# First MLP of an attention and two-MLP kernel: results leave and return by ScalarE's DMA queue, work between products becomes chains

## The chip, the cores and the metric

The kernel runs on one core of a Trainium2 chip. The metric is the device time of one execution in microseconds (us), the median of several runs. TensorE (PE in the profile) multiplies matrices and accumulates in PSUM banks; VectorE (DVE) and ScalarE (ACT) do element-wise passes; SyncE (SP) issues DMAs. Each engine works through its own queue of instructions in order, and an engine whose next instruction waits holds everything behind it.

## The reference

```python
attn = phi(q) @ (phi(k).T @ v) / den        # linear attention, 4 x 8 heads, 576 tokens
x = attn as 2304 x 512
h = x @ w_in;  g = np.maximum(0.01 * h, h);  x = g @ w_out          # first MLP, 512 -> 2048 -> 512
h = x @ w_in2; g = h * np.tanh(softplus(h)); out = g @ w_out2       # second MLP, same sizes
```

Weights come as 64-bit floats and the result is to have 32-bit accuracy.

## The kernel before

**Products.** A product of 32-bit floats is made of three matmuls of high and low halves (`three`, L96 to L99: high with high, high with low, low with high). The halves come from a ScalarE copy (`high`, the L201 and L93 passes) and a VectorE subtraction (`low`, L205 and L94). Weights are first converted from 64-bit floats: a load into a `stage` place (L124, two places, 512 KB each, by SP), a clamp and a shift on VectorE (L135, L137), a scale on ScalarE (L141), two joining passes on VectorE (L146 into a scratch tile `e`, L150 into `c`). There are two `c` places. A converted block is used at once or stored to DRAM (`scr`, L159, SP) and fetched later (`fc`, L164, SP).

**First MLP, in-stage.** Blocks f = 0 to 7 of w_in and two halves of the tokens make 16 items. An item is seven products of six 128x512 matmuls each in the manner of Strassen (`cycle`, L860); per f there is also a product for the 256 left-over tokens (`c_item`, 24 matmuls of 256 columns). Between products stand small passes on which the next product waits: copies of banks by ScalarE (`seed_y` L657, `keep_p7` L660) and sums of banks by VectorE (L704, L709). A finished result goes through `leaky` (L694): a ScalarE pass into one of six 256 KB places (`g`), then a DMA to DRAM (L698, `gd<-g`, SP). There are 72 results.

**First MLP, out-stage.** Five blocks of tokens (512, 512, 256, 512 and 512 columns) in 16, 16, 8, 16 and 16 steps. A step (`emit_y`, L922) is 12 matmuls of 512 columns (24 of 256 in the short block) on one result, which comes back by a DMA (`load_g`, L913, `raw<-gd`, SP) and is cut into `gh` (ScalarE) and `gl` (VectorE) by `split_g`, two steps ahead. The loads stand four steps ahead, in the last block two steps ahead. In the last block each step also fetches and splits a w_out block of the second MLP (`swap`, L1126), and the second MLP's first products begin.

**What sets the order.** Weight work for later stands in one list of pieces (`piece`, L608; `conv_pieces`, L800; `w_pieces`, L790). After some products `work` (L618) takes pieces from the head of the list while tokens last: four calls in a `cycle`, one in an out-stage step, each call worth 1.75 to 2.4 us of VectorE work. `need` (L622) takes pieces until the one that a product wants is out. All DMAs of these stages stand in SP's queue, in program order.

Of the kernel before, what the change touches and what calls it, by code (L numbers as in the profile page):

```python
# [23 lines left out]
def attention_two_mlps_kernel(  # L24
# [39 lines left out]
    NC = B * LEFT  # L64

# [41 lines left out]
    class Loads:  # L107


        def __init__(self, units):  # L110
            self.units, self.at, self.stage = units, 0, {}

        def load(self, ahead=1):
            while self.at < len(self.units) and len(self.stage) <= ahead:
# [10 lines left out]
                self.stage[which, m, x] = stg  # L125

    def conversion(u, then):
# [64 lines left out]
    def w_sums(f):  # L192
        c0, c1 = kept[0, 2 * f, 0], kept[0, 2 * f + 1, 0]
        l0, r0, l1, r1 = c0[:, 0:E], c0[:, E:], c1[:, 0:E], c1[:, E:]
        for o, x, op, y in ((r1, l1, ALU.add, r1), (l1, l0, ALU.subtract, l1),
                            (l0, r1, ALU.subtract, l0), (r0, r0, ALU.subtract, l0)):
            nc.vector.tensor_tensor(out=o, in0=x, in1=y, op=op)
# [42 lines left out]
    with tc.manual_schedule():  # L240
# [253 lines left out]
        def attention(n):  # L494
# [48 lines left out]
            if n == PAIRS - 1:  # L543
# [9 lines left out]
        l1_order = {}  # L553
        for f in range(3, NF):
            part = -(-len(others) // (NF - f))
            l1_order[f] = others[:part] + [(0, 2 * f, 0), (0, 2 * f + 1, 0)]
            others = others[part:]
        l2_order = out1[DIRECT + STORED:] + [(1, m, 0) for m in range(M)] + out2[AHEAD:]
        loads = Loads([u for u, _ in att_units.values()] + [u for x in l1_order.values() for u in x] + l2_order)
        conv = {n: conversion(u, then(u)) for n, (u, then) in att_units.items()}  # L560
# [45 lines left out]
        gd, ready, bg, tokens, rate, free = {}, {}, [], [0.0], [1.9], set()  # L606

        def piece(cost, f, mark=None, gate=None):  # L608
            bg.append((cost, f, gate))
            if mark is not None:  # L610
                ready[mark] = f

        def next_piece():
            cost, f, gate = bg.pop(0)
            assert gate is None or gate in free
            f()
            return cost
# [70 lines left out]
        turn = [0]  # L688

        def staged():  # L690
            turn[0] += 1
            return work6(("ta", "gh", "gl")[turn[0] % 3], "g", F32)

        def leaky(key, h):  # L694
            g = staged()
            nc.scalar.activation(out=g, in_=h, func=AF.Prelu, alpha=0.01)
            gd[key] = dr.tile([P, MAIN], F32, name="gd%d_%d" % key)
            nc.sync.dma_start(out=gd[key], in_=g)  # L698

        def tail5(n):  # L700
# [4 lines left out]
            leaky((2 * x["f"] + 1, 2 * x["sb"] + 1), c)  # L705
# [52 lines left out]
        def high_piece(part):  # L758
            piece(0.0, lambda: high(part()))

        def low_piece(cost, part, mark):
            piece(cost, lambda: low(part()), mark)

        c_part = lambda: cw + [XC]
        x1 = lambda o: (lambda: x_part(1, o))
        high_piece(c_part)
        low_piece(1.22, c_part, ("x", "c", 0))
        high_piece(x1(B11))
        piece(0.69, lambda: nc.vector.tensor_tensor(out=XC[:, 0:2], in0=XC[:, 2:4], in1=XC[:, 0:2], op=ALU.subtract))
        high_piece(d_part)  # L770
        low_piece(1.22, x1(B11), ("x", 1, B11))
        low_piece(0.69, d_part, ("x", "c", 1))
        high_piece(x1(B22))
        piece(1.22, lambda: x_sum(1, T1))
        piece(1.22, lambda: x_sum(1, T3))
        high_piece(x1(T3))
        low_piece(1.22, x1(B22), ("x", 1, B22))
        piece(1.22, lambda: x_sum(1, T2))
        high_piece(x1(T2))
        low_piece(1.22, x1(T3), ("x", 1, T3))  # L780
# [416 lines left out]
```

## Time and profile before

| | us |
|---|---|
| median of three runs (1031.61 to 1036.34) | 1032.63 |
| profiled execution, its own time | 1036.78 |
| its span | 1034.9 |
| TensorE busy | 972.4 |
| VectorE busy | 727.4 |
| ScalarE busy | 528.4 |

The stages in the profiled execution: attention to 176.6 us, the in-stage of the first MLP to 395.4, its five out blocks to 446.7, 493.6, 518.0, 565.0 and about 645, then the second MLP to the end. A busy TensorE is not one at its peak: the granted clock has two levels, and a stretch after idle time can stand at the lower one.

### The profile page before, as it was taken

To read this page: it belongs to the slowest core of one execution; us is meant where nothing else is said; L and a number is where in the kernel's file an instruction comes from. 1 tells how busy PE (TensorE), PEld (TensorE's weight loads), DVE (VectorE), ACT (ScalarE), POOL (GpSimd) and SP (SyncE) were. 2 spreads that over 40 slices of the span, in tenths; PEclk is the share of its full clock that TensorE was granted. 3 is DMA by queue.
4 is the path that set the end of the run, shared out by engine and by line. 5 is a ranking of instruction groups with operands and counts; after the bars stand their busy time and mean duration, and the time that the engine had idled before them with its cause. 6 is when DMAs were issued, how large, how long until landed. Compare 5 with 4: busy or idle time off the path is not lost.

```text
span 1034.9 us, 16987 instructions
## 1 busy us (share of the span) xinstructions
PE 972.4 (94%) x6645; PEld 810.9 (78%) x6645; DVE 727.4 (70%) x1282; ACT 528.4 (51%) x898; POOL 68.7 (7%) x36
## 2 busy tenths in 40 slices
PE   8999999978968898999999879999999999999998
PEld 7889998766757786767977547888888988888886
DVE  7888995757665313777876224987886888868975
ACT  6888896644444333444443223645544555445543
POOL 4444431000000000000000000000000000000000
PEclk9999999999989899999999889999999999999999
DMA  7534411237765325656577222000100100000001
GB/s 196 142 86 119 128 46 43 83 132 223 233 194 181 136 112 176 213 181 202 194 259 229 96 91 79 11 1 1 41 1 1 41 1 21 1 1 35 7 0 41
DMA packets 84367, 102.88 MB, mean 99 GB/s; under 512 B 28992, under 2 KB 53952, under 8 KB 84288
## 3 DMA queue, kind: packets, MB, share of 16 engines
q1 hardware_dynamic: 83552, 101.41, 30.8%
q8 instruction: 52, 0.85, 0.4%
q10 hardware_dynamic: 736, 0.39, 0.1%
q14 instruction: 27, 0.22, 0.1%
HBM read 72.42 MB, written 29.36 MB: 98 GB/s over the span
## 4 chain that ended last, share of the span: by engine, by line
PE 58%; DVE 11%; DMA 9%; ACT 5%; issue 4%; SPq 1%; ACTq 0%; DVEq 0%
PE b L97 10%; PE b L98 9%; PE b L99 9%; PE a L97 9%; PE a L98 9%; PE a L99 9%; DMA scr<-c 4%; DMA raw<-gd 4%; DVE e L146 2%; DVE c L150 2%; DVE gl L94 2%; ACT gh L93 2%; DVE c L135 1%; PE outs L432 1%; PE kvp L409 1%
## 5 line engine op out<-in xcount | busy, mean ns | idle before, releaser
L98 PE MATMUL a<-win,wi 128*128 128x512 f32 (+1 forms) x320 | 117.7, 368 | 0.0
L99 PE MATMUL a<-win,wi 128*128 128x512 f32 (+1 forms) x320 | 117.7, 368 | 0.0
L97 PE MATMUL a<-win,wi 128*128 128x512 f32 (+1 forms) x320 | 117.7, 368 | 0.0
L99 PE MATMUL b<-wo,gl 128*128 128x512 f32 x288 | 112.2, 390 | 0.4 <-DVE gl L1044 0.4
L97 PE MATMUL b<-wo,gh 128*128 128x512 f32 x288 | 112.2, 389 | 0.0
L98 PE MATMUL b<-wo,gh 128*128 128x512 f32 x288 | 112.2, 389 | 0.0
L94 DVE TENSOR_TENSOR gl<-raw,gh 128x512 fp32r<-128x512 f32 x72 | 49.6, 689 | 83.3 <-ACT gh L93 83.2
L97 PE MATMUL b<-gh,wo 128*128 128x512 f32 (+1 forms) x192 | 72.7, 379 | 16.7 <-ACT gh L93 16.3
L141 ACT ACTIVATE c<-c 128x512 f32<-128x512 f32 x64 | 40.5, 633 | 90.9 <-DVE c L135 89.4
L1026 ACT ACTIVATE gh<-u 128x512 fp32r<-128x512 f32 x72 | 45.5, 633 | 69.8 <-PE b L98 63.0
L93 ACT ACTIVATE gh<-raw 128x512 fp32r<-128x512 f32 x72 | 44.8, 623 | 70.2 <-DMA raw<-gd 57.1
L98 PE MATMUL b<-gl,wo 128*128 128x512 f32 (+1 forms) x192 | 73.7, 384 | 4.0 <-DVE gl L94 3.7
L392 POOL PARTITION_ALL_REDUCE qm<-qd x32 | 68.5, 2189 | 90.8 <-ACT qd L387 77.2
L99 PE MATMUL b<-gh,wo 128*128 128x512 f32 (+1 forms) x192 | 71.1, 370 | 0.1
L1053 ACT ACTIVATE r<-e,two 128x512 f32<-128x512 f32 x72 | 51.7, 718 | 37.0 <-DVE e L1038 37.0
L97 PEld LDWEIGHTS a<-win,wi 128*128 128x128 f32 x320 | 60.3, 188 | 10.3
L98 PEld LDWEIGHTS a<-win,wi 128*128 128x128 f32 x320 | 60.3, 188 | 10.3
L99 PEld LDWEIGHTS a<-win,wi 128*128 128x128 f32 x320 | 60.3, 188 | 10.1
L1022 ACT ACTIVATE e<-a 128x512 f32<-128x512 f32 x72 | 43.0, 597 | 47.1 <-PE a L99 26.3
L99 PEld LDWEIGHTS b<-wo,gl 128*128 128x128 f32 x288 | 54.1, 188 | 12.5 <-DVE gl L1044 1.2
L97 PEld LDWEIGHTS b<-wo,gh 128*128 128x128 f32 x288 | 54.1, 188 | 11.0
L98 PEld LDWEIGHTS b<-wo,gh 128*128 128x128 f32 x288 | 54.1, 188 | 10.9
(223 smaller groups left out, 2364.1 us busy)
## 6 DMA issues: line engine op xcount, KB each, us to landing
gd<-g SPq DMA_DIRECT2D x72, 256.0 KB, 2.0
raw<-gd SPq DMA_DIRECT2D x72, 256.0 KB, 4.0
stage<-in_moe_w_in_dram SPq DMA_DIRECT2D x32, 512.0 KB, 3.9
stage<-in_moe_w_out_dram SPq DMA_DIRECT2D x32, 512.0 KB, 4.1
scr<-c SPq DMA_DIRECT2D x22, 256.0 KB, 4.3
fc<-scr SPq DMA_DIRECT2D x19, 256.0 KB, 2.7
qn<-in_q_dram SPq DMA_DIRECT2D x16, 256.0 KB, 3.9
vmain<-in_v_dram SPq DMA_DIRECT2D x32, 128.0 KB, 3.0
```

Source lines behind the costliest of these rows:

```text
L93: nc.scalar.activation(out=hi, in_=src, func=AF.Copy)
L94: nc.vector.tensor_tensor(out=lo, in0=src, in1=hi.bitcast(F32), op=ALU.subtract)
L97: nc.tensor.matmul(out=o, lhsT=wh_, rhs=xh, start=start, stop=False, **kw)
L98: nc.tensor.matmul(out=o, lhsT=wh_, rhs=xl, start=False, stop=False, **kw)
L99: nc.tensor.matmul(out=o, lhsT=wl_, rhs=xh, start=False, stop=stop, **kw)
L141: nc.scalar.activation(out=box["c"], in_=box["c"], func=AF.Copy, scale=2.0 ** -112)
L146: nc.vector.scalar_tensor_tensor(out=e, in0=stg[:, :, 1], scalar=-(1 << 31), in1=stg[:, :, 0], op0=ALU.bitwise_and, op1=ALU.bitwise_or)
L150: nc.vector.scalar_tensor_tensor(out=c.bitcast(I32), in0=c.bitcast(I32), scalar=3, in1=e, op0=ALU.logical_shift_left, op1=ALU.bitwise_or)
L392: nc.gpsimd.partition_all_reduce(qm, qd, P, bass_isa.ReduceOp.absmax)
L1022: nc.scalar.activation(out=e0, in_=h0, func=AF.Exp)
L1026: nc.scalar.activation(out=hi2, in_=u2, func=AF.Copy)
L1053: nc.scalar.activation(out=r0, in_=e0, func=AF.Ln, bias=two)
```

## The change

- `leaky` no longer issues its DMA; the DMA is put aside (`sent`) and issued on ScalarE's queue at the next call of `work`, one product later. `load_g` issues on ScalarE's queue too, six steps ahead instead of four (the first six loads come before the last item of the in-stage); in the last block two at a time every second step, the last six into `stage` places.
- `work` is called once per product (seven times per item, twice per out-stage step). The list of pieces becomes a queue of chains; each call lets every open chain (at most four) do one stage at most, and tokens are worth 1.3 us per call, 1.0 in the out-stage.
- `c` has three places. A clamp is placed at the earliest three calls after the load of its block was issued (`landed`). The scratch tile `e` is gone: L146's result is written into the `stage` place, which is given back after L150 instead of after L146.
- 31 conversions stand in the in-stage instead of 24: for each f three blocks go to the store beside the two of w_in. The last two of the seven conversions in the attention stage now store w_out blocks; they kept w_in blocks. Blocks of w_out that the first MLP needs are fetched from the store, four of them before the handover between the stages. Two calls of `drain` empty the queue: at the handover, and one step before the last block.
- Up to three pairs `gh`, `gl` are made ahead instead of two. `swap` keeps three fetches in flight instead of two.

```diff
+    CS, LAND = 3, 3
...
-            c = box["c"] = gp.tile([P, DM], F32, tag="c", name="c")
+            c = box["c"] = gp.tile([P, DM], F32, tag="c", name="c", bufs=CS)
...
             stg, c = box["s"], box["c"]
-            e = gp.tile([P, DM], I32, tag="w1", name="e", bufs=1)
-            nc.vector.scalar_tensor_tensor(out=e, in0=stg[:, :, 1], scalar=-(1 << 31), in1=stg[:, :, 0],
+            e = stg[:, :, 0]
+            nc.vector.scalar_tensor_tensor(out=e, in0=stg[:, :, 1], scalar=-(1 << 31), in1=e,
                                            op0=ALU.bitwise_and, op1=ALU.bitwise_or)
+            nc.vector.scalar_tensor_tensor(out=c.bitcast(I32), in0=c.bitcast(I32), scalar=3, in1=e,
+                                           op0=ALU.logical_shift_left, op1=ALU.bitwise_or)
             del loads.stage[u]
             loads.load()
-            nc.vector.scalar_tensor_tensor(out=c.bitcast(I32), in0=c.bitcast(I32), scalar=3, in1=e,
-                                           op0=ALU.logical_shift_left, op1=ALU.bitwise_or)
             then(c)
...
-    def fetch(u, tag="c"):
-        c = gp.tile([P, DM], F32, tag=tag, name="f" + tag, **({"bufs": 1} if tag == "w1" else {}))
+    def fetch(u):
+        c = gp.tile([P, DM], F32, tag="c", name="f", bufs=CS)
         nc.sync.dma_start(out=c, in_=scr[u])
         return c
...
-        DIRECT, STORED, AHEAD = 3, 5, 6
-        att_units = {1: ((0, 0, 0), keep), 2: ((0, 1, 0), keep), 5: ((0, 0, 1), store), 7: ((0, 2, 0), keep),
-                     8: ((0, 3, 0), keep), 15: ((0, 4, 0), keep), 16: ((0, 5, 0), keep)}
-        out1, out2 = [(0, m, 1) for m in range(1, M)], [(1, m, 1) for m in range(M)]
-        others = out1[:DIRECT + STORED] + out2[:AHEAD]
...
+        ATT = {1: ((0, 0, 0), keep), 2: ((0, 1, 0), keep), 5: ((0, 0, 1), store), 7: ((0, 2, 0), keep),
+               8: ((0, 3, 0), keep), 15: ((0, 1, 1), store), 16: ((0, 2, 1), store)}
+        HERE, EARLY, EACH = 4, 1, 3
+        out1, out2 = [(0, m, 1) for m in range(M)], [(1, m, 1) for m in range(M)]
+        spare = out1[3:] + out2
...
+        for f in range(2, NF + 1):
+            part = EARLY if f == 2 else EACH
+            pair = [(0, 2 * f + i, 0) for i in range(2) if f < NF]
+            l1_order += pair + spare[:part] if f == 2 else spare[:part] + pair
+            spare = spare[part:]
+        l2_order = [(1, m, 0) for m in range(M)] + spare
...
-        gd, ready, bg, tokens, rate, free = {}, {}, [], [0.0], [1.9], set()
...
-        def work(share=1.0):
-            tokens[0] = min(tokens[0] + share * rate[0], 2.0 * rate[0])
-            while bg and tokens[0] > 0 and (bg[0][2] is None or bg[0][2] in free):
-                tokens[0] -= next_piece()
+        gd, free, undone, pos, tokens, rate = {}, set(), set(), [0], [0.0], [1.3]
+        queue, active, sent = [], [], []
+        loads.pos = pos
...
+            def step(self, force):
+                x = self.stages[0]
+                if pos[0] < self.at + x.after and not force:
+                    return
+                if (x.gate is not None and x.gate not in free) or (x.ok is not None and not x.ok(force)):
+                    return
+                if x.cost > 0 and tokens[0] <= 0 and not force:
+                    return
+                self.at = pos[0]
+                tokens[0] -= x.cost
+                self.stages.pop(0)
+                x.f()
+                undone.discard(x.mark)
...
+        def work(force=False):
+            pos[0] += 1
+            while sent:
+                sent.pop(0)()
+            tokens[0] = min(tokens[0], 0.0) + rate[0]
+            for x in list(active):
+                x.step(force)
+            active[:] = [x for x in active if x.stages]
+            while queue and len(active) < 4 and not any(x.open() for x in active) and (force or queue[0].begin <= pos[0]):
+                x, n = queue[0], len(queue[0].stages)
+                x.at = -9
+                x.step(force)
+                if len(x.stages) == n:
+                    return
+                queue.pop(0)
+                if x.stages:
+                    active.append(x)
...
-            f = ready.pop(mark, None)
-            while f is not None and any(f is x for _, x, _ in bg):
-                next_piece()
+            while mark in undone:
+                work(True)
...
+        def drain():
+            while queue or active:
+                work(True)
...
+        turn, stage_tags = [0], [("ta", "gh", "gl")]
         def staged():
             turn[0] += 1
-            return work6(("ta", "gh", "gl")[turn[0] % 3], "g", F32)
-        def leaky(key, h):
-            g = staged()
+            return work6(stage_tags[0][turn[0] % len(stage_tags[0])], "g", F32)
+        def leaky(key, h, g=None):
+            g = staged() if g is None else g
             nc.scalar.activation(out=g, in_=h, func=AF.Prelu, alpha=0.01)
             gd[key] = dr.tile([P, MAIN], F32, name="gd%d_%d" % key)
-            nc.sync.dma_start(out=gd[key], in_=g)
+            sent.append(lambda: nc.scalar.dma_start(out=gd[key], in_=g))
...
-        def conv_pieces(u, then):
-            c, s, j = conversion(u, then)
-            piece(0.85, lambda: (c(), s()))
-            piece(1.38, j)
...
+        def room(force=False):
+            return len(held) < CS or held[-CS][0]
...
+        def landed(u):
+            def ok(force):
+                loads.load()
+                return room() and u in loads.stage and (force or pos[0] >= loads.when[u] + LAND)
+            return ok
...
+        def to_store(u):
+            box, st_ = conv_stages(u)
+            j = st_[2]
+            f = j.f
+            j.f = drop(box, lambda: (f(), store(u)(box["out"])))
+            chain(*st_)
...
+        def from_store(u, begin=0):
+            box = {}
+            def get():
+                box["h"] = hold()
+                box["out"] = fetch(u)
+            h, l = into_home(u, box)
+            h.after = LAND
+            chain(Stage(0.0, get, ok=room, last=True), h, l, begin=begin)
...
-            t = rawt[s] = place("a%d" % (s % RAW), F32, MAIN, name="raw") if s < LAST else work6("ta", "raw")
-            nc.sync.dma_start(out=t, in_=gd[steps[s][2]])
+            if s < LAST + 10:
+                t = place("a%d" % (s % RAW), F32, MAIN, name="raw")
+            else:
+                if (s - LAST) % 2 == 0:
+                    raw2[0] = gp.tile([P, 2, MAIN], F32, tag="stage", name="raw2")
+                t = raw2[0][:, s % 2]
+            rawt[s] = t
+            nc.scalar.dma_start(out=t, in_=gd[steps[s][2]])
...
+        def g_tag(s):
+            return s % 3 == 2 and s < NS - 6
...
-            hi, lo = work6("gh", "gh"), work6("gl", "gl")
+            hi, lo = ((work6("ta", "gh", F32R), work6("ta", "gl", F32R)) if g_tag(s) else (work6("gh", "gh"), work6("gl", "gl")))
...
+        def splits(s):
+            while s + 3 >= len(gs) < NS:
+                x = len(gs)
+                before = [y for y in gs if g_tag(y) == g_tag(x)][-1 if g_tag(x) else -2:]
+                if len(before) == (1 if g_tag(x) else 2) and before[0] > s:
+                    return
+                gs.append(x)
+                split_g(x)
...
+                if n == len(it) - 1:
+                    for s in range(6):
+                        load_g(s)
...
-        while bg:
-            next_piece()
-        for s in range(4):
-            load_g(s)
+        drain()
+        for u in out1[HERE:]:
+            from_store(u)
...
+        rate[0] = 1.0
...
             h, l = home[1, m, 1] = home_of((1, m, 1))
             split(h, l, box2.pop(m))
-            x = m + 2 if m + 2 <= M - 3 else m + 1
-            if M - 3 != m + 1 and x < M:
-                box2[x] = fetch(out2[x], "c" if x < M - 3 else "w1")
+            if m + CS < M:
+                box2[m + CS] = fetch(out2[m + CS])
...
         def l2_step(s):
-            emit_y(s)
-            if s < LAST - 4:
-                load_g(s + 4)
-            elif s >= LAST - 2:
-                load_g(s + 2)
-            split_g(s + 2)
+            emit_y(s, 0, 1)
             work()
+            emit_y(s, 2, 3)
+            splits(s)
+            if s < LAST + 4:
+                load_g(s + 6)
+            elif (s - LAST) % 2 == 0:
+                load_g(s + 6)
+                load_g(s + 7)
+            work()
+            if s >= LAST:
+                swap(s - LAST)
         for s in range(NS):
-            if s == LAST - 2:
-                while bg:
-                    next_piece()
+            if s == LAST - 1:
+                drain()
```

SP's queue in the second half of the in-stage; `stage` is a load of a 64-bit block, `scr` a store of a converted one, `gd` a result. Before:

```order
L698 DMA gd_3_3570<-g 128x512
L164 DMA fc<-scr_0_1_1314 128x512
L124 DMA stage<-in_moe_w_out_dram 128x1024
L698 DMA gd_2_3605<-g 128x512
L124 DMA stage<-in_moe_w_in_dram 128x4x256 x2
L698 DMA gd_3_3654<-g 128x512
```

After:

```order
L161 DMA scr_6_1_3703<-c 128x512
L125 DMA stage<-in_moe_w_out_dram 128x1024 x3
L161 DMA scr_7_1_3833<-c 128x512
L125 DMA stage<-in_moe_w_in_dram 128x4x256
L161 DMA scr_8_1_3886<-c 128x512
```

The results are gone from SP's queue; loads and stores of weights alone are left.

VectorE's queue near the end of the in-stage: 14 conversion passes stand in a row ahead of a sum of banks (`g<-b,z`, `b<-b,z`) on which TensorE waits; `z` is the copy that `keep_p7` makes, `x_...` a low half of a weight. Before, the end of that row:

```order
L146 SCALAR_TENSOR_TENSOR e<-stage 128x512
L150 SCALAR_TENSOR_TENSOR c<-c,e 128x512
L135 TENSOR_SCALAR c<-stage 128x512
L137 TENSOR_SCALAR stage<-stage 128x512
L704 TENSOR_TENSOR g<-b,z_74 128x512
L709 TENSOR_TENSOR b<-b,z_75 128x512
```

After, at the same sums:

```order
L747 TENSOR_TENSOR g<-b,z_74 128x512
L207 TENSOR_TENSOR x_0_4184<-c,x_0_4184 128x512
L137 TENSOR_SCALAR c<-stage 128x512
L139 TENSOR_SCALAR stage<-stage 128x512
L752 TENSOR_TENSOR b<-b,z_75 128x512
L207 TENSOR_TENSOR x_1_4198<-c,x_1_4198 128x256
L199 TENSOR_TENSOR c<-c 128x256 x4
L148 SCALAR_TENSOR_TENSOR stage<-stage 128x512
L150 SCALAR_TENSOR_TENSOR c<-c,stage 128x512
```

The conversions are cut up between the sums.

The last out block: SP's queue before, where each return of a result (`raw<-gd`) stands behind a fetch:

```order
L164 DMA fc<-scr_6_1_6119 128x512
L913 DMA raw<-gd_3_4145 128x512
L164 DMA fc<-scr_7_1_6166 128x512
L913 DMA raw<-gd_3_4408 128x512
L164 DMA fc<-scr_8_1_6195 128x512
```

and ScalarE's queue after:

```order
L1017 DMA raw_6578<-gd_3_4606 128x512
L1017 DMA raw_6578<-gd_3_4567 128x512
L94 ACTIVATE wo<-f 128x512
L94 ACTIVATE gh<-raw 128x512
```

The returns stand in pairs on ScalarE; SP's queue keeps the fetches alone.

## Rows read from the trace of the kernel before

**Rows 1.** Stretches by stage: start:end length, busy us (instructions) of PE, PEld, DVE, ACT, POOL; clock.
```profile
176.60:395.40 218.80, 189.70 (x856) 155.90 (x852) 114.38 (x197) 95.76 (x166) 0.00 (x0) 0.92 0.49 163
395.40:446.70 51.30, 46.80 (x193) 35.45 (x194) 33.90 (x60) 21.10 (x37) 0.00 (x0) 1.00 0.54 180
446.70:493.60 46.90, 45.60 (x194) 35.32 (x192) 37.21 (x66) 21.66 (x37) 0.00 (x0) 1.00 0.59 192
493.60:518.00 24.40, 23.61 (x193) 23.12 (x192) 20.63 (x38) 11.78 (x21) 0.00 (x0) 1.00 0.61 201
518.00:565.00 47.00, 45.93 (x194) 35.48 (x193) 33.21 (x62) 17.20 (x31) 0.00 (x0) 1.00 0.78 253
565.00:644.90 79.90, 65.58 (x230) 47.39 (x230) 26.79 (x44) 23.12 (x42) 0.00 (x0) 0.89 0.28 92
645.00:1000.00 355.00, 354.65 (x1655) 297.15 (x1654) 290.38 (x490) 181.61 (x291) 0.00 (x0) 1.00 0.04 12
```

**Rows 2.** TensorE's waits in the in-stage: us in total, times, longest.
```profile
PE b L97 <- ACT b L657: 14.8, 5, 5.4
PE b L97 <- DVE g L704: 9.9, 4, 4.8
PE a L97 <- DVE g L704: 2.3, 1, 2.3
```

**Rows 3.** TensorE's waits in the first four out blocks (395.4 to 565).
```profile
PE b L97 <- ACT gh L93: 4.3, 3, 2.3
```

**Rows 4.** TensorE's waits in the last out block (565 to 644.9).
```profile
PE b L97 <- ACT gh L93: 12.0, 10, 1.8
```

**Rows 5.** Timeline: start, length; first matmuls of two stretches twelve matmuls apart.
```profile
219.85 0.39 PE L97 MATMUL a<-v,a 128*128 128x512 f32 x1
...
222.57 0.39 PE L97 MATMUL b<-s,x 128*128 128x512 f32 x1
```

**Rows 6.** Ten microseconds after a stall, columns as in rows 1.
```profile
230.00:240.00 10.00, 9.74 (x32) 7.29 (x32) 8.55 (x16) 5.55 (x11) 0.00 (x0) 0.72 0.66 200
```

**Rows 7.** Timeline of one stall in the in-stage; in brackets idle before and its releaser.
```profile
257.01 0.43 DVE L135 TENSOR_SCALAR c<-stage 128x512 f32<-128x512 f32 x1 [1.81 <-DMA scr<-c]
...
257.47 0.63 ACT L141 ACTIVATE c<-c 128x512 f32<-128x512 f32 x1 [3.46 <-DVE c L135]
...
259.62 0.79 PE L97 MATMUL b<-v,x 128*128 128x512 f32 x1 [3.69 <-ACT b L657]
```

**Rows 8.** VectorE's waits in the in-stage.
```profile
DVE c L135 <- DMA scr<-c: 16.5, 10, 2.3
```

**Rows 9.** Waits of SP's queue, 185 to 640.
```profile
SPq L698 <- ACT g L696: 125.7, 59, 5.8
SPq L164 <- DVE wo L94: 50.2, 11, 5.4
```

**Rows 10.** Timeline of one step of the last block.
```profile
587.33 0.32 SPq L164 DMA_DIRECT2D fc<-scr  x1
587.70 0.42 SPq L913 DMA_DIRECT2D raw<-gd  x1
590.75 0.63 ACT L93 ACTIVATE gh<-raw 128x512 fp32r<-128x512 f32 x1 [3.73 <-DMA raw<-gd]
```

**Rows 11.** DMA issues from 190 to 345: count, KB each, median us to landing.
```profile
stage<-in_moe_w_out_dram SPq DMA_DIRECT2D x14, 512.0 KB, 4.3
```

**Rows 12.** DMA issues on ScalarE's queue at the program's start.
```profile
0.75 0.39 ACTq L276 DMA_DIRECT2D kn<-in_k_dram  x1
...
3.24 1.38 ACTq L289 DMA_DIRECT2D ql<-in_q_dram  x2
```

**Rows 13.** Groups of VectorE's instructions in the in-stage: busy us, mean ns.
```profile
L146 DVE SCALAR_TENSOR_TENSOR e<-stage 128x512 int32<-128x512 int32 x24 | 16.6, 692 | 0.7
...
L135 DVE TENSOR_SCALAR c<-stage 128x512 f32<-128x512 f32 x24 | 10.2, 423 | 16.5 <-DMA scr<-c 16.5
```

**Rows 14.** Groups of ScalarE's instructions in the in-stage.
```profile
L696 ACT ACTIVATE g<-b 128x512 f32<-128x512 f32 x31 | 18.4, 595 | 19.4 <-PE b L99 17.4 <-ACT g L696 1.5 <-ACT x L201 0.2
```

More of the change, by code (lines that the diff above doesn't have):

```diff
@@ new lines, in attention_two_mlps_kernel, with __init__, open @@
+        class Chain:
+            def __init__(self, stages, begin=0):
+                self.stages, self.begin, self.at = list(stages), begin, pos[0]
+                undone.update(x.mark for x in stages if x.mark is not None)
+            def step(self, force):
[11 more added lines that the diff above has]
+                undone.discard(x.mark)
+            def open(self):
+                return any(not x.last for x in self.stages)
@@ L800, in conv_pieces, with row, f @@
-        def conv_pieces(u, then):
-            c, s, j = conversion(u, then)
-            piece(0.85, lambda: (c(), s()))
-            piece(1.38, j)
+        def row(cost, *todo, mark=None):
+            def f():
+                for t in todo:
+                    t()
+            return Stage(cost, f, mark)
+        hi_ = lambda part: (lambda: high(part()))
+        lo_ = lambda part: (lambda: low(part()))
+        sum_ = lambda o: (lambda: x_sum(1, o))
+        d_sub = lambda: nc.vector.tensor_tensor(out=XC[:, 0:2], in0=XC[:, 2:4], in1=XC[:, 0:2], op=ALU.subtract)
@@ new lines, in attention_two_mlps_kernel, with hold, conv_stages, c_ @@
+        held = []
+        def room(force=False):
+            return len(held) < CS or held[-CS][0]
+        def hold():
+            held.append([False])
+            return held[-1]
+        def landed(u):
[3 more added lines that the diff above has]
+            return ok
+        def conv_stages(u, last=True):
+            box = {}
+            c, s, j = conversion(u, lambda x: box.update(out=x))
+            def c_():
+                box["h"] = hold()
+                c()
+            return box, [Stage(0.85, c_, ok=landed(u), last=last), Stage(0.0, s), Stage(1.38, j)]
@@ new lines, in drop, with g, w_chain, got @@
+        def drop(box, f=None):
+            def g():
+                if f is not None:
+                    f()
+                box["h"][0] = True
+            return g
+        def w_chain(f, begin):
+            b0, (c0, s0, j0) = conv_stages((0, 2 * f, 0))
+            b1, (c1, s1, j1) = conv_stages((0, 2 * f + 1, 0), last=False)
+            sums = [lambda: w_sums(f, slice(0, 2)), lambda: w_sums(f, slice(2, 4))]
+            p = lambda i: (lambda: w_part(f, i))
+            def got():
+                kept[0, 2 * f, 0], kept[0, 2 * f + 1, 0] = b0["out"], b1["out"]
+            def both(*fs):
+                def g():
+                    for x in fs:
+                        x()
+                return g
+            c1.after = 1
+            chain(c0, Stage(0.85, both(s0.f, c1.f), ok=c1.ok, last=False), Stage(1.38, both(j0.f, s1.f)), Stage(1.38, both(j1.f, got)),
+                  Stage(0.0, hi_(p(0)), gate=(f - 2, 0)),
+                  Stage(0.69, both(lo_(p(0)), hi_(p(1))), ("w", f, 0), gate=(f - 2, 1)),
+                  Stage(1.27, both(lo_(p(1)), sums[0]), ("w", f, 1)),
+                  Stage(0.84, both(sums[1], hi_(p(2))), gate=(f - 2, 2)),
+                  Stage(0.69, both(drop(b1, lo_(p(2))), hi_(p(3))), ("w", f, 2), gate=(f - 2, 3)),
+                  Stage(0.69, drop(b0, lo_(p(3))), ("w", f, 3)), begin=begin)
@@ L842, in out_w @@
             return home[u]
-        w_pieces(2)
-        from_store((0, 0, 1))()
-        for f in range(3, NF):
-            for u in l1_order[f]:
-                if u[2] == 0:
-                    conv_pieces(u, keep(u))
-                elif u in out1[:DIRECT]:
-                    direct(u)
-                else:
-                    conv_pieces(u, store(u))
-            w_pieces(f)
+        begin = {2: 13, 3: 28}
+        begin.update((f, 22 + 16 * (f - 3)) for f in range(4, NF))
+        todo = list(l1_order)
+        while todo:
+            u = todo.pop(0)
+            if u[2] == 0:
+                todo.pop(0)
+                w_chain(u[1] // 2, begin[u[1] // 2])
+            else:
+                to_store(u)
+        for m in range(HERE):
+            from_store(out1[m])
         def used(n, *parts):
@@ L882, in cycle @@
             head2(n)
+            work()
             tail3(n - 1)
@@ L933, in emit_y @@
                           start=(m == 0), stop=(m == M - 1))
+            if KD - 1 not in ds:
+                return
+            del gt[s]
             if ms[-1] == M - 1:
```

164 lines of the change are left out of this document (59 added, 105 removed).

## The prediction

> **What bounds the kernel now.** I read the stretches by stage first: each row gives a stage's length beside its TensorE busy time and clock [rows 1]. From 645 to 1000 us TensorE is busy for 354.65 of 355.00 us at full clock; the change leaves that stage alone, so it keeps its time. The first MLP, 176.6 to about 645, is another matter: in-stage and last block have both idle time and a clock under 1. I price each stage by what its matmuls need back to back. Twelve matmuls of 512 columns, one step, take 222.57 - 219.85 = 2.72 us, 0.2267 each [rows 5]. For 256 columns I take the short block's busy time, 23.61 / 193 = 0.122 [rows 1].
>
> - In-stage: by the code 108 products of 6 matmuls and 8 of 24 narrow ones: 648 x 0.2267 + 192 x 0.122 = 170.3, with 1.5 us set aside for its 16 other matmuls 171.8, against 218.80. Excess 47.0.
> - First four out blocks: 3 x 192 x 0.2267 + 192 x 0.122 = 154.0 against 51.30 + 46.90 + 24.40 + 47.00 = 169.6. Excess 15.6.
> - Last block: 230 x 0.2267 = 52.1 against 79.90. Excess 27.8.
>
> Together 90.4 us, all that better order can win. Which waits make it up? In the in-stage TensorE waits 14.8 us for the ScalarE copy that seeds a bank and 9.9 + 2.3 for the VectorE sum [rows 2]; in the last block 12.0 for `gh` [rows 4]; in the four blocks between 4.3 for it [rows 3]. Idle time alone is less than the excess: the in-stage's idle is 218.80 - 189.70 = 29.1. The other 18 are the clock: in the ten microseconds from 230 us TensorE was busy for 9.74, yet 32 matmuls ran instead of 10 / 0.2267 = 44, at a granted 0.72, a mix of the levels 2.4 and 1.2 GHz [rows 6]. So a stall is paid more than once here, and its removal returns more than its idle time.
>
> One stall shows the mechanism [rows 7]. VectorE's clamp waits 1.81 us for a store to read its `c` place; ScalarE's scale waits 3.46 us for that clamp; the seed copy stands behind the scale in ScalarE's queue, and TensorE waits 3.69 us for it. The store was itself late in SP's queue, whose results wait 125.7 us in all for their ScalarE pass [rows 9]. VectorE waited for such stores ten times, 16.5 us [rows 8]. In the last block the same happens on SP alone: the fetch waits for a VectorE pass over its place (50.2 us over 11 fetches), the result's return stands behind the fetch, is issued at 587.70, and its `gh` begins at 590.75, after 3.73 us of idle [rows 9, 10].
>
> **The change part by part.**
>
> *Results' DMAs to ScalarE.* 72 out and 72 back leave SP. A DMA issue on ScalarE took 0.39 us for one and 1.38 for two [rows 12]; so 0.39 to 0.69. Per f (14 products and one narrow item, 14 x 1.36 + 24 x 0.122 = 22.0 us of TensorE) ScalarE does some 22 passes (9 results, 4 copies, 5 scales, 4 halves) at about 0.6 [rows 14] = 13.2, and 9 issues add 3.5 to 6.2: 16.7 to 19.4 of 22.0. It fits, and since the issue is put off by one product, the pass it reads is long done: price nothing, with 2.6 us per f as cover. What is queued behind such an issue is the next seed copy, so 0.69 us of its slack goes. In the out-stage a step has 0.6 for `gh`, up to 1.2 for weights and 0.69 for the load, 2.5 of 2.72, and `gh` is made two steps ahead.
>
> *Chains, one stage per product.* This removes the cause of [rows 7] and of the waits for the sum: of 14 conversion passes in a row, about 14 / 2 x (0.423 + 0.692) = 7.8 us [rows 13] ahead of a sum, at most a few stay between two sums. VectorE's load per f is now five conversions of 2 x 0.423 + 2 x 0.692 = 2.23, so 11.1; lows 3 x 0.69 + 0.42 = 2.5; four sums of weights 1.7; four sums of banks 2.8: 18.1 of 22.0 us. Half widths are priced as the clamp's 0.423, an estimate.
>
> *The added wait.* A clamp now follows its load by three calls, some 4.1 us of TensorE work (3 x 1.36), while a load took 4.3 to land as a median [rows 11]. Queued behind a clamp that waits are the sums on VectorE, and the scale and then the seed copy on ScalarE. Price from both sides: nothing (the load lands in time), or 2 us, the worst wait of a clamp before, near the 2.3 of [rows 8]. I take 0.2 us per conversion, since the distance misses the median by that. 18.1 + 1 = 19.1 of 22.0 still fits, but not evenly, since some products carry two conversion passes and a sum; I leave 10 of the 47.0 us: about 1.2 us for each of six f, and 3 for the beginning, where the halves of the other tokens are made.
>
> *Three `c` places, `e` in place.* A `c` place comes back one conversion later, so the 16.5 us of [rows 8] go. The `stage` place comes back 0.69 us later, one L150 [rows 13]; that is in the 0.2 us above.
>
> *Handover.* `drain` puts a fetch and its split on ScalarE in a row ahead of the last item's passes, without lead. A fetch is like the return in [rows 10]: 590.75 - 587.70 = 3.05, and 0.63 for the split. I add 4 us.
>
> *Out blocks.* 33 conversions become 26, and two calls of 1.0 per step bound VectorE to about 2 us of weights and 0.69 for `gl` per 2.72 us. That is nearly full; the lead of two to three steps hides single lumps. I leave 2 us in the first block and 3 in the other three, 5 of 15.6.
>
> *Last block.* The return no longer stands behind the fetch, and is issued six steps ahead; nothing of the loop of [rows 10] is left. VectorE has 0.69 for `gl`, 0.69 for a fetched half and a few splits: half of a step. I leave 2 of 27.8 us.
>
> A rule speaks against half of this. The last block is where only the queue changes, and there the DMA share is 0.28 [rows 1], so what was short was a turn in SP's queue, not the engines that move data. The Trainium skill (DMA: Bandwidth & Descriptors, "Issuing engines are not separate DMA queues") says that transfers started by several engines run on the same 16 DMA engines, and that starting them on more engines saves only the time of the issue. By that the last block would keep its excess; the 50.2 us in [rows 9] are a wait at the issue, before any transfer, which that rule doesn't count.
>
> Sum: 10 + 4 + 5 + 2 = 21 of 90.4 stay, 69.4 go. 1036.78 - 69.4 = 967.4 for a profiled execution; that of before lay 4.15 above the median of its runs, so **963**.
>
> **The rivals.**
>
> *A, VectorE becomes the bound.* Each of the 31 conversions of the in-stage waits the full 2 us for its load. Then VectorE has 18.1 + 10 = 28.1 per f against 22.0, six f lose 37 instead of 10, and the out blocks 8 instead of 5 (loads 3 calls ahead there too). Excess 37 + 4 + 8 + 2 = 51, saved 39.4: 993. For it: the distance is under the median landing time, and two `stage` places allow no earlier load. Against it: SP's queue is rid of the results, and landing is counted from issue with DMA shares of 0.49 to 0.78, part of which are lumps that even spacing takes away. Range 976 to 1000.
>
> *B, the queue is worth nothing.* The returns land no earlier, since the transfers are what is late: 26 of the last block's excess stay, the rest goes as forecast. 10 + 4 + 5 + 26 = 45, saved 45.4: 987. That is the rule above; against it speak the share of 0.28 and the 3.05 us that one return took once it was issued.
>
> *C, slower: ScalarE pays the issues.* If an issue holds ScalarE until its transfer has been taken over, at x us each, an f costs 13.2 + 9x against 22.0 and a step 1.5 + x against 2.72. Over eight f and 72 steps that is 144x - 158 us; it eats all that is saved elsewhere (69 + what it replaces, about 80) from x = 1.65 on. At x = 2 it is 130 on top of the 946.4 that back-to-back matmuls leave, with 10 for the rest: 1086, less 4.15, 1082. Against it: 0.39 to 0.69 in [rows 12]; for it: no row has such an issue in a busy ScalarE queue.
>
> *D, it does not do what it says.* The order shows the conversions spread between the sums and the returns on ScalarE, so only a new stall of the same size elsewhere would leave the time within 0.5%.
>
> **How the numbers follow.** Forecast 0.71 (945 to 976), A 0.18, B 0.05, C 0.04, D 0.02. The floor is 946.4 - 4.15 = 942 if all excess goes; the handover alone makes that unlikely, so the range begins at 945, with 3 us left. It ends at 990: that takes in B and nearly half of A, and leaves the rest of A with C and D, about 0.2 together with the tails of the forecast. A measurement of this kernel can tell about 0.5% from no change. Faster by more than that: 0.71 + 0.18 + 0.05 = 0.94; same 0.02; slower 0.04.
>
> **What would show it.** Right: in-stage about 186 us at a granted clock near 1, the sums and seed copies gone from TensorE's waits, four out blocks of 159, a last block of 54 to 56 with no wait for `gh`. A shows as VectorE waiting at the clamp for `stage` loads, over 1 us each, and TensorE behind it. B shows as ScalarE's `gh` waiting for `raw` in the last block although the load was issued early. C shows as DMA issues of over a microsecond on ScalarE and TensorE waiting for ScalarE's passes. I am wrong in the in-stage if its clock stays near 0.9: then many short waits do what a few long ones did.

## The result

The changed kernel takes 1024.89 us (median of 4 runs, 1022.09 to 1025.09) against 1032.79 (1031.61 to 1036.34): a ratio of 0.991, 95% interval 0.988 to 0.994. Eight microseconds were won where 69 were forecast. The stretches by stage of the changed kernel, with the columns of [rows 1], show where:

```profile
176.60:394.00 217.40, 189.08 (x859) 152.07 (x854) 126.48 (x227) 101.27 (x174) 0.00 (x0) 0.94 0.61 202
394.00:442.40 48.40, 45.47 (x195) 37.08 (x193) 28.25 (x50) 21.21 (x38) 0.00 (x0) 0.96 0.56 180
442.40:501.80 59.40, 48.85 (x193) 37.70 (x192) 40.16 (x74) 23.17 (x40) 0.00 (x0) 0.94 0.54 160
501.80:531.10 29.30, 25.26 (x194) 24.68 (x192) 18.59 (x35) 10.20 (x18) 0.00 (x0) 0.94 0.66 212
531.10:580.80 49.70, 47.21 (x194) 37.99 (x193) 22.39 (x39) 13.66 (x24) 0.00 (x0) 0.93 0.60 181
580.80:632.90 52.10, 52.10 (x231) 43.13 (x231) 24.95 (x40) 21.82 (x39) 0.00 (x0) 1.00 0.42 122
```

The last block is at its floor: 231 matmuls in 52.1 us, 27.8 us less than in [rows 1]. The in-stage kept its length, 217.4 after 218.8. The four blocks between became longer, 186.8 after 169.6. What TensorE waits for (us, times, longest) in the in-stage:

```profile
PE b L98 <- ACT b L700: 10.4, 4, 5.2
PE b L98 <- DVE g L747: 7.9, 4, 2.9
```

and in the four blocks:

```profile
PE a L99 <- DVE gl L95: 11.8, 8, 3.2
PE b L99 <- DVE gl L95: 7.0, 3, 3.5
```

The seed copy (L700, then L657) and the sum (L747, then L704) are still there [rows 2], and `gl`, a VectorE pass, takes the place of `gh` [rows 3]. What VectorE itself waits for, 176 to 640 us:

```profile
DVE c L137 <- DMA stage<-in_moe_w_in_dram: 48.9, 17, 4.5
DVE c L137 <- DMA stage<-in_moe_w_out_dram: 36.8, 21, 3.0
```

The clamp waits 85.7 us for loads of 64-bit blocks, 46.5 of them in the in-stage and 39.2 in the four blocks. The waits for stores of [rows 8] are gone, and this wait stands where they stood, several times as long. (One wait of VectorE is longer than either row, 51.2 us for `gh`; in the four blocks it is 25.8 us, and 32.2 before, so it is no newcomer.) One piece of the timeline of the second block (start, length; idle before and releaser in brackets) joins the two:

```profile
456.01 2.30 SPq L125 DMA_DIRECT2D stage<-in_moe_w_in_dram  x2
...
457.22 0.69 DVE L150 SCALAR_TENSOR_TENSOR c<-c,stage 128x512 int32<-128x512 int32 x1
...
460.35 0.42 DVE L137 TENSOR_SCALAR c<-stage 128x512 f32<-128x512 f32 x1
...
464.85 0.43 DVE L137 TENSOR_SCALAR c<-stage 128x512 f32<-128x512 f32 x1 [3.75 <-DMA stage<-in_moe_w_in_dram]
...
465.53 0.69 DVE L95 TENSOR_TENSOR gl<-raw,gh 128x512 fp32r<-128x512 f32 x1
...
466.27 0.50 PE L99 MATMUL a<-gl,wo 128*128 128x512 f32 x1 [3.16 <-DVE gl L95]
```

Two conversions run side by side and hold both `stage` places. Each place comes back after its L150, and the second load goes out at about 457.9, 1.9 us behind the first. It lands just before the clamp at 464.85, after nearly 7 us. VectorE stands at the clamp for 3.75 us, `gl` is queued behind it, and TensorE waits 3.16 us for `gl`.

### The profile page after: what moved, and what is told of

Same layout as the page of the kernel before. It is cut to its first block, busy times and chain, and to the rows that moved or that the text cites. A ratio compares the mean times of both kernels' runs of the same rounds, so it can differ in the third digit from the quotient of the medians.

```text
span 1022.9 us, 16911 instructions
## 1 busy us (share of the span) xinstructions
PE 962.8 (94%) x6645; PEld 810.4 (79%) x6645; DVE 722.6 (71%) x1282; ACT 529.8 (52%) x898; POOL 68.7 (7%) x36
## 4 chain that ended last, share of the span: by engine, by line
PE 55%; DMA 16%; DVE 12%; issue 2%; ACT 1%; ACTq 0%; DVEq 0%; SPq 0%
PE a L98 9%; PE a L100 9%; PE b L98 9%; PE a L99 9%; PE b L100 9%; PE b L99 9%; DMA stage<-in_moe_w_in_dram 8%; DMA stage<-in_moe_w_out_dram 7%; DVE stage L148 3%; DVE c L150 2%; DMA f<-scr 2%; DVE gl L95 1%; PE outs L434 1%; DVE stage L139 1%; DVE c L199 1%
## 5 line engine op out<-in xcount | busy, mean ns | idle before, releaser
L95 DVE TENSOR_TENSOR gl<-raw,gh 128x512 fp32r<-128x512 f32 x72 | 49.5, 689 | 58.6 <-ACT gh L94 51.2
L137 DVE TENSOR_SCALAR c<-stage 128x512 f32<-128x512 f32 x64 | 27.2, 424 | 85.7 <-DMA stage<-in_moe_w_in_dram 48.9
L99 PE MATMUL b<-gl,wo 128*128 128x512 f32 (+1 forms) x192 | 69.7, 363 | 7.0 <-DVE gl L95 7.0
L100 PE MATMUL b<-gh,wo 128*128 128x512 f32 (+1 forms) x192 | 69.3, 361 | 0.0
L98 PE MATMUL b<-gh,wo 128*128 128x512 f32 (+1 forms) x192 | 69.2, 360 | 0.0
L1142 ACT ACTIVATE e<-a 128x512 f32<-128x512 f32 x72 | 43.0, 597 | 47.8 <-PE a L100 26.6
L99 PE MATMUL a<-gl,wo 128*128 128x512 f32 x128 | 53.5, 418 | 11.9 <-DVE gl L95 11.8
```

What stands on the lines that cost most here:

```text
L95: nc.vector.tensor_tensor(out=lo, in0=src, in1=hi.bitcast(F32), op=ALU.subtract)
L98: nc.tensor.matmul(out=o, lhsT=wh_, rhs=xh, start=start, stop=False, **kw)
L99: nc.tensor.matmul(out=o, lhsT=wh_, rhs=xl, start=False, stop=False, **kw)
L100: nc.tensor.matmul(out=o, lhsT=wl_, rhs=xh, start=False, stop=stop, **kw)
L137: nc.vector.tensor_scalar(out=c, in0=stg[:, :, 1].bitcast(F32), scalar1=F64_TOP, scalar2=-F64_TOP, op0=ALU.min, op1=ALU.max)
L1142: nc.scalar.activation(out=e0, in_=h0, func=AF.Exp)
```

## Theories and experiments

**Load theory.** Two `stage` places, held until the second joining pass, give loads that come late; VectorE stands at the clamp, and what is queued behind it holds TensorE. In a narrow form the distance of three calls is too short, in a wide one the pace of the two places is. **Amount theory**: 31 conversions are too much work for VectorE in the in-stage. **Issue theory** (a small rival C): 144 DMA issues hold ScalarE. For the last block a **queue theory** stands against a **lead theory**. Twelve kernels ran; medians of before in the three groups were 1035.8, 1033.9 and 1035.1, so times of kernels of different groups are compared to some 3 us at best. Stage lengths are from one profiled run each: in-stage, four blocks, and from the last block to the end of the span. Before, these are 219, 170 and 470; after, 217, 187 and 442.

### The last block: queue or lead

`last_queue`, the kernel before with one edit:

```diff
-            nc.sync.dma_start(out=t, in_=gd[steps[s][2]])
+            (nc.sync if s < LAST else nc.scalar).dma_start(out=t, in_=gd[steps[s][2]])
```

> The kernel before, with one edit: in the last out block the returns of results (raw<-gd) are issued on ScalarE's queue instead of SP's; they stay two steps ahead. Queue theory (the return is late because it stands behind the fetch on SP): last block 80 -> 54 to 60 us, total about 1010. Lead theory (what helps in the changed kernel is the six steps of lead): the return now stands right ahead of its own gh on ScalarE, so each step still pays its landing of about 3 us plus two ScalarE passes, some 4.2 us per step against 5.3 before: last block 67, total about 1020. If the transfers themselves were late: no change, 1033.

Measured 1011.2 us, ratio 0.976 (0.972 to 0.979); stages 218, 170, 446. This one line beats the whole change. In its last block:

```profile
587.77 0.63 ACT L93 ACTIVATE gh<-raw 128x512 fp32r<-128x512 f32 x1 [1.48 <-DMA raw<-gd]
587.82 0.33 ACTq L913 DMA_DIRECT2D raw<-gd  x1
...
590.72 0.63 ACT L93 ACTIVATE gh<-raw 128x512 fp32r<-128x512 f32 x1 [1.79 <-DMA raw<-gd]
```

A return issued at 587.82 has its `gh` at 590.72: the 3 us of [rows 10], but now one such turn follows the other, without the fetch, and the last block takes 56.9 us. The queue theory holds; the lead theory's 4.2 us per step was wrong, since the next return is issued while the passes of this step run.

`results_on_sp`, the changed kernel with both DMAs of results on SP again:

```diff
-            sent.append(lambda: nc.scalar.dma_start(out=gd[key], in_=g))
+            sent.append(lambda: nc.sync.dma_start(out=gd[key], in_=g))
...
-            nc.scalar.dma_start(out=t, in_=gd[steps[s][2]])
+            nc.sync.dma_start(out=t, in_=gd[steps[s][2]])
```

> The changed kernel with results out and back on SP's queue again; chains, places, lead and amounts stay. If ScalarE pays for the 144 issues (rival C in small): in-stage and out blocks get shorter, total under 1020. If the queue made the gain of the last block: it loses 20 us there, total about 1045. If the lead made it: total within 5 us of the changed kernel's 1025.

1017.4 us, 0.982 (0.979 to 0.985); stages 217, 178, 442. The stretch from the last block on is at 442 on either queue. So the queue alone cures the last block, and the rest of the change (six steps of lead, three fetches in flight instead of two) cures it without the queue. The lead was not run by itself.

ScalarE's queue cost 7.5 us, nearly all in the four blocks (187 against 178). The issue theory forecast this, but the traces point elsewhere. In the changed kernel two returns go out on ScalarE's queue 0.1 and 0.6 us after the second load of a pair; in `results_on_sp` they stand behind it on SP's own queue. The landing times of twelve loads of the second block, first the changed kernel (434 to 492 us), then `results_on_sp` (430 to 484):

```profile
DMA to landing us min/median/max: 3.5/4.7/6.8
DMA to landing us min/median/max: 3.8/4.5/5.5
```

With the returns on SP the second load lands 5.0 to 5.6 us after its issue instead of 5.7 to 6.8, and a pair of conversions takes 10.1 us from clamp to clamp instead of 11.1. That speaks for returns that hold up the loads, and not for ScalarE's time; no run tried the two apart.

### The early release

`early_release`: from the in-stage on, sign and low word are joined right behind the clamp, into a scratch place taken from the results' places, and the `stage` place goes back there.

```diff
...
+            if late[0] is not None:
+                e = box["e"] = late[0].tile([P, DM], I32, tag=e_tag[0], name="e")
+                nc.vector.scalar_tensor_tensor(out=e, in0=stg[:, :, 1], scalar=-(1 << 31), in1=stg[:, :, 0],
+                                               op0=ALU.bitwise_and, op1=ALU.bitwise_or)
+                del loads.stage[u]
+                loads.load()
...
```

> The changed kernel, but from the in-stage on a conversion joins sign and low word right behind the clamp (into one of two scratch places taken from the results' places, which become four; pairs gh, gl two ahead instead of three), so a stage place is given back 1.5 us of VectorE work after its load is first read, and the next load starts a scale and two calls earlier. VectorE's work is the same. Load theory (two stage places, held for three calls, pace the conversions and VectorE's clamp waits for the load): clamp waits fall from 86 us to under 40, in-stage 217 -> about 195, first four out blocks 185 -> about 165, total about 985. Amount theory (31 conversions are too much work for VectorE in the in-stage): nothing changes, 1020 to 1030.

982.7 us, 0.950 (0.947 to 0.952); stages 204, 159, 442. Its stretches:

```profile
176.60:380.20 203.60, 184.48 (x861) 151.71 (x858) 127.40 (x227) 100.50 (x174) 0.00 (x0) 0.95 0.65 216
380.20:424.00 43.80, 43.78 (x194) 35.82 (x193) 31.59 (x56) 23.04 (x41) 0.00 (x0) 1.00 0.72 218
```

and its waits for loads at the clamp:

```profile
DVE c L137 <- DMA stage<-in_moe_w_out_dram: 10.7, 8, 2.1
DVE c L137 <- DMA stage<-in_moe_w_in_dram: 5.7, 4, 2.0
```

VectorE does the same passes on the same blocks, the DMA share is higher, and the waits fall from 85.7 to 16.4 us and the time by 42. That is the load theory; one of the joining passes moves to the clamp's call with the release, and what that alone is worth was not run. The loads themselves are no faster: as medians they land in 4.4 and 4.8 us, 5.0 and 4.5 in the changed kernel.

`scratch_back` gives the place back one joining pass sooner, as the kernel before did, and pays with a `c` place; the last block's fetches are two ahead again, as before:

```diff
-    CS, LAND = 3, 3
+    CS, LAND = 2, 3
...
-            e = stg[:, :, 0]
+            e = gp.tile([P, DM], I32, tag="w1", name="e", bufs=1)
...
```

> The changed kernel with the scratch tile of the conversion back and two c places: a stage place is given back 0.69 us earlier (before the second joining pass), a c place comes back one conversion sooner needed. Load theory: 31 + 26 conversions each get their load 0.7 us earlier; by half of that up to 15 us are won, unless the c places take it: 1010 to 1025. If three c places were what the change lived on, clamps wait for stores again as in the kernel before: 1030 to 1045.

1025.3 us, 0.992 (0.990 to 0.995), as the changed kernel; stages 224, 180, 442. Part of the wait moves back to stores (47.8 us of the in-stage's clamp waits). This tells nothing between the theories: one place was paid with another.

`before_release` makes the same early release in the kernel before.

```diff
...
+            if late[0] is not None:
+                first()
...
```

> The kernel before (one list of pieces, results on SP, two c places), with one edit from the in-stage on: sign and low word are joined right behind the clamp, so the stage place goes back one scale and one piece earlier. VectorE's waits there were for c places (19 us) and not for loads. If the chains are what makes an early release worth much: within 5 us of 1033. If the release alone is the gain of early_release and chains give nothing: about 1000.

1032.7 us, 0.998 (0.997 to 0.999); stages 219, 165, 468. The release alone is worth 2 us where conversions stand in rows. The in-stage and the four blocks lose 16 us by the chains (results and all) without the release, and win 26 with it: with the clamp three calls behind its load, neither pays without the other. With five calls the chains do pay without the release, as the next kernel shows.

### Distance and amount

`clamp_later`:

```diff
-    CS, LAND = 3, 3
+    CS, LAND = 3, 5
```

> The changed kernel with a clamp at the earliest five calls after its load was issued instead of three (fetches from the store too). Load theory in its narrow form (TensorE waits because VectorE stands at a clamp whose load has not landed, three calls being too few): clamp waits fall from 86 us to under 30 and the total to about 1000. In its wide form (the pace of two stage places is what is short, and early_release won by giving them back sooner): a place is now held longer, so conversions come later and are forced out by the products that need them: total 1015 to 1035.

999.0 us, 0.966 (0.963 to 0.969); stages 217, 161, 443. The time is the narrow form's, but its clamp waits are not: 50.0 us stay. In the four blocks, with TensorE's longest wait there:

```profile
DVE c L137 <- DMA stage<-in_moe_w_out_dram: 17.9, 9, 3.4
DVE c L137 <- DMA stage<-in_moe_w_in_dram: 15.1, 9, 3.7
PE a L99 <- DVE gl L95: 2.1, 5, 0.7
```

VectorE waits 33.0 us for loads in the blocks, hardly less than the 39.2 of the changed kernel, and yet the blocks are cured: TensorE's waits for `gl` fall from 18.8 to 2.9 us. In the in-stage it is the other way round: the clamp's waits fall from 46.5 to 15.8 us, and the stage does not move. So the wait at the clamp is not by itself what TensorE pays for. VectorE's order shows what is. These are the `gl` passes from the first clamp of one pair of conversions to that of a later pair, in the changed kernel (438.4 to 504.9 us, six pairs), `clamp_later` (446.0 to 508.8, six pairs) and `early_release` (408.4 to 465.1, seven pairs):

```profile
L95 DVE TENSOR_TENSOR gl<-raw,gh x18: 683/685/694, 442.5 to 503.7; 128x512 fp32r<-128x512 f32 x18
L95 DVE TENSOR_TENSOR gl<-raw,gh x21: 681/685/694, 446.7 to 507.9; 128x512 fp32r<-128x512 f32 x21
L95 DVE TENSOR_TENSOR gl<-raw,gh x21: 681/691/695, 409.8 to 463.9; 128x512 fp32r<-128x512 f32 x21
```

A step of TensorE needs one `gl` and takes 2.72 us [rows 5]. In the changed kernel the program puts three `gl` between two pairs, and a pair takes 11.1 us, the turn of the two places: 3.7 us per `gl`, and TensorE has to follow. With five calls three and four `gl` stand there by turns, and a pair takes 10.5 us: 3.0 us per `gl`, near enough, it seems, for the pairs made ahead to cover the rest. With the early release the turn itself is short: 8.1 us for a pair and three `gl`, 2.7 each. This is the wide form's cause, the pace of the two places, though its forecast for this kernel was wrong: more calls let more steps pass per turn.

`fewer_in_stage`:

```diff
-        HERE, EARLY, EACH = 4, 1, 3
+        HERE, EARLY, EACH = 4, 1, 2
```

> The changed kernel with two blocks per f instead of three sent to the store in the in-stage: 25 conversions there, the other six in the out blocks. Amount theory (31 conversions are too much for VectorE in the in-stage): in-stage 217 -> 195 us, out blocks at most 5 us longer, total about 1008. Load theory (a stage place comes back late, so conversions go at about 5 us each wherever they stand, and what waits behind a clamp waits with it): what the in-stage gains by up to 20 us the out blocks lose, total 1018 to 1030.

1012.3 us, 0.979 (0.975 to 0.982); stages 194, 197, 442. Six conversions less take 24 us off the in-stage, as the amount theory said, and put 10 on the blocks, more than it allowed. `later_fewer` has both numbers:

> The changed kernel with two numbers changed: a clamp five calls behind its load, and two blocks per f to the store instead of three; no early release. clamp_later won 26 us over the changed kernel, fewer_in_stage 13. If they cure different stretches (the one the out blocks, the other the in-stage): the gains add, about 986, in-stage near 194 and out blocks near 161. If both act through the pace of two stage places: not more than the better one, 995 to 1005.

```diff
-    CS, LAND = 3, 3
+    CS, LAND = 3, 5
...
-        HERE, EARLY, EACH = 4, 1, 3
+        HERE, EARLY, EACH = 4, 1, 2
```

999.6 us, 0.966 (0.963 to 0.969); stages 189, 163, 471. The gains of the stages do add, and 28 us come back elsewhere, most of it in one wait at the last block's start:

```profile
PE b L98 <- ACT gh L94: 23.0, 1, 23.0
```

`drain` stands there: conversions that did not get through in time are made in one go while TensorE idles. With five calls of distance two places do not get all blocks through. So it is the pace in both stretches. In the blocks more steps per turn help, as long as the conversions still get through in time; in the in-stage fewer or faster conversions are needed.

### What beats both kernels

Four kernels stand on `early_release`. `early_fewer`:

```diff
-        HERE, EARLY, EACH = 4, 1, 3
+        HERE, EARLY, EACH = 4, 1, 2
```

> early_release (983 us) with two blocks per f to the store instead of three. Its in-stage is 204 us against 172 back to back; four of its stalls of 2.5 to 3.3 us come behind clamps that wait for a load or a store, one of 5.0 us behind a fetch at the handover. Amount theory for what is left: fewer conversions, less in VectorE's and the stores' way, and the fetches come out before the queue is drained: in-stage about 190, out blocks up to 3 us longer, total about 972. If the pace of loads and stores still sets it: 980 to 990.

964.2 us, 0.932 (0.929 to 0.936); stages 181, 161, 442. The in-stage:

```profile
176.60:357.80 181.20, 174.63 (x857) 145.26 (x854) 115.58 (x203) 97.32 (x168) 0.00 (x0) 1.00 0.64 216
```

Against `early_release` idle time falls from 19.1 to 6.6 us and the stage by 22.4: the rest is the clock, 1.00 after 0.95.

`early_on_sp` is `early_release` with the edit of `results_on_sp`:

> early_release (983 us) with results out and back on SP's queue. results_on_sp won 8 us over the changed kernel, all in the out blocks, where its VectorE waited less for gh. If issuing from ScalarE itself costs (144 issues of 0.3 to 0.45 us ahead of gh and seed copies): total about 976. If ScalarE's turn matters only while VectorE is held by clamps: 983 within 4. If SP's queue is held by stores and loads that wait: results come late, over 987.

977.4 us, 0.946 (0.942 to 0.949); stages 196, 159, 442. One premise of this expectation is wrong: VectorE did not wait less for `gh` in the four blocks of `results_on_sp`, but 34.5 us against 25.8.

`early_fewer_sp` is `early_fewer` with that edit too:

> early_fewer (964 us) with results out and back on SP's queue, as early_on_sp won 5 us on early_release. If ScalarE's issues cost by themselves: about 959. If they only cost while the in-stage is too full: 964 within 2.

962.9 us, 0.931 (0.929 to 0.934), the fastest, though not clear of `early_fewer`; stages 178, 163, 442. SP's queue is worth 7.5, 5.4 and 1.3 us in the three pairs. The first is clear of the noise, the second barely, the third is not; the first lies in the four blocks, the second in the in-stage. That ScalarE's queue costs the more, the less slack there is, fits the three, but is not shown, nor is what was late in the second pair.

`early_fewer_later` is `early_fewer` with one number more:

```diff
-    CS, LAND = 3, 3
+    CS, LAND = 3, 4
```

> early_fewer with a clamp at the earliest four calls after its load instead of three. Its clamps still wait 14.8 us for loads. Narrow form (VectorE standing at a clamp is what holds TensorE): waits fall under 8 and 1 to 3 us are won, 962. If the pace is short again: conversions come too late, 965 to 975.

965.3 us, 0.933 (0.930 to 0.936). Clamp waits for loads stay (16.2 us), nothing is won: with the early release three calls are enough.

## Why the prediction was wrong

963 was forecast, 945 to 990, and 1024.9 came. Rival A, given 0.18, is what happened, and its own price was too low as well.

- **Last block.** Right: 25.8 us off were forecast, 27.8 came, and the return behind the fetch is its cause (`last_queue`). `last_queue` won 23 us with the queue alone, at the same transfers; what ended was a wait at the issue. The Trainium skill (DMA: Bandwidth & Descriptors, "Issuing engines are not separate DMA queues") says that starting transfers on more engines saves only the time of the issue. By that rule the queue would have been worth no more than that; the measurement decides. That B got a small chance was right.
- **The added wait.** This is the step that failed: 0.2 us per conversion, taken from three calls of TensorE's work (4.1 us) against a median landing of 4.3 [rows 11]. Measured: 38 waits, 85.7 us, 1.5 us for each of the 57 conversions. Three things were wrong in it. VectorE is not tied to TensorE's calls; it works ahead, and the distance on its own queue is what it finds to do, as the timeline shows. Two conversions run together, so their loads go out 1.9 us apart, and the second lands late (464.85 after about 457.9, near 7 us). And a place is held through the spread that the chains bring: the 0.69 us that I put "in the 0.2 us above" was the small part of it. Nor is the wait itself the price, as `clamp_later` shows. What the sum has no term for is the turn of the two places: 11.1 us for a pair in the second block, in which the order lets three steps pass that need 8.2 us.
- **Chains.** The mechanism was right, its gain was not to be had at the pace that the two places allowed. Forecast 37 us of the in-stage and 10.6 of the blocks; `early_release`, which keeps the chains, has 159 in the blocks, the forecast's own number, but 204 in the in-stage against "about 186". `early_fewer` has 181 there, with 25 conversions instead of the 31 that were priced.
- **Out blocks.** 5 us of excess were left, 32.8 came. "Nearly full" counted VectorE's passes, and the lead was to hide single lumps; here pair after pair of conversions was late, by the same missing term.
- **31 conversions.** I called 19.1 of 22.0 us per f a fit. Of VectorE's busy time that holds, but its waits were not in it; with 25 the in-stage alone was 24 us shorter.
- **ScalarE's issues.** Priced at nothing. Results on SP's queue won 7.5 us (`results_on_sp`), by earlier landings of the second loads as far as the traces show, which no term of the prediction has. C in full size did not come: single issues took 0.33 us.
- **Handover.** 4 us forecast. The longest wait of the in-stage, 5.2 us for the seed copy at 370 us, stands there behind the fetches: the step held.
- **A.** Its 2 us per wait was the right size (85.7 / 38 = 2.3). It counted them in the in-stage alone and gave the blocks 3 us more; there VectorE waited 39 us, and the blocks' excess is 186.8 - 154.0 = 32.8, not 8. That is most of where 993 falls short of 1025; another 4 us are the 4.15 taken off for a profiled execution, which here lay only 0.1 above its median. What spoke for it, a distance under the median landing time, I had written down and then priced by the difference of two medians.

## What to carry to other kernels

When a load's place is given back by the work that it feeds, price the whole turn of the place (load, wait, every pass until it is free) against the pace at which the work is wanted; count the consumer's steps that the program puts into one turn, for they must last at least as long. A wait on the engine that does this work is a sign and not the price: two more calls of distance left 33 of 39 us of it and cured the blocks. Spreading work in small steps holds its places longer, so look for the pass after which a place is dead and move it first. For a transfer that is late, see first whether it waits at its issue: then one line that changes the queue can be worth all of it, as here. And look at what else goes out with a load: here a return on another queue seems to have made it late.

## What was not expected of the hardware

A return issued on ScalarE's queue took 0.33 us of it (587.82 above), the low end of [rows 12] and under it. Loads of 512 KB landed in 4.4 to 5.0 us as medians at DMA shares from 0.54 to 0.83; the medians did not rise with the share. Of two sent off 1.9 us apart, the second took near 7 us in the piece shown, with two returns of 256 KB started on ScalarE's queue just after it; where these stood behind it on SP's queue, it took 5.0 to 5.6.
